# Moving one key-value block per pass next to the P blocks, and the ends of phi's softmax into the left places

## The chip, the cores and the metric

The kernel runs on one core of a Trainium2 chip. The metric is the device time of one execution in microseconds. A core has TensorE (matrix products; PE in the profile, its weight loads PEld), DVE (VectorE, elementwise work and reductions), ACT (ScalarE, activation functions and copies), POOL (GpSimd, used here for a few transfers) and SP (SyncE, which issues most transfers). Matmuls write to PSUM, which has eight banks.

## The reference

Attention through 32 memory slots for each head, then a feed-forward network with Silu, all in float32:

```python
a   = softmax(phi, axis=memory)             # 8 batches, 8 heads, 576 positions, 32 slots
k_m = einsum('bhsm,bhsd->bhmd', a, k)       # keys and values gathered into the slots
v_m = einsum('bhsm,bhsd->bhmd', a, v)
attn = softmax(q @ k_m.T / sqrt(64))        # 576 x 32 for each head
x   = attn @ v_m                            # then (4608, 512)
h   = x @ w_in                              # (4608, 2048)
out = (h * sigmoid(h)) @ w_out              # (4608, 512)
```

## The kernel before

Each of the eight batches is one pass over its 576 rows. For a batch the kernel multiplies the values with the input weights first (P = v_m times w_in, tile pm, four blocks of 512 columns), so that the first layer of the network is attention (tile aparts) times P. Every operand of a large product is split into a high and a low float32r part, and three of the four products of parts are added up.

A pass has 16 places, numbered 0 to 15. In passes 2 to 7 a place is one *step*: `ffn1s` makes h, the Silu input, for two chunks of 128 columns and half of the rows (12 matmuls at L846); `forms` evaluates Silu on ACT (L858, L860) and makes the operands of the second layer on ACT and DVE (L869 to L881); the place's other work (`run`) is issued; then `finish` issues the second layer of the step before (`st_step`, 21 matmuls at L894). That layer uses Strassen's seven products instead of eight; the combined weights it needs, `kept`, are made once from the sum of the weight parts (`w_sums` fetches that sum by transfers on POOL's queue, `w_forms` combines and splits it on DVE and ACT) in the course of passes 1 and 2. Pass 0 and the first ten places of pass 1 use plain products.

512 of the 576 rows of each batch go through these steps. The other 64 rows of two successive batches are kept in gleft and worked through together at the end of passes 1, 3, 5 and 7, in four *left places* with the numbers 16 to 19: `left_split` copies and splits a quarter of gleft (L978 on ACT, L979 on DVE), `run` issues the place's other work, and `finish` issues the matmuls of the *preceding* left part (`left_st`, L996). The fourth left part's matmuls come in the first step of the next pass.

Beside this, pass b prepares batch n = b + 1. Its pieces are put into the places by `ev(pass, place, function, ...)`, for passes 2 to 6 in `steady`:

- phi's softmax: `phi_max` and the three steps of `phi_fold` find a maximum on DVE, `phi_sub` subtracts it (DVE, L312 and L315), `phi_exp` takes the exponential (ACT, L319). Exponential and Silu are in different tables of ACT, so each exponential has a table load ahead of it and another one behind.
- `e_mm`, the key-value block: 80 small matmuls on 32-column tiles of TensorE (L335, L345), then rs and kvn on DVE and ACT (L353 to L361). It writes to the tile bg (`banks`) or to unused columns beside h (`beside_h`).
- `e_tr` and `s_all`: transposes and the scores (L382), which DVE turns into sc (L389, L391); then the softmax `s_max` ... `s_norm`; then `s_back` turns sc back (L464, DVE), `s_high` copies the high part into aparts (L472, ACT) and `s_low` the low part (L479, DVE).
- `p_mm`, a P block: 16 matmuls on 32-column tiles (L648) to bg or to two tiles pacc, then a copy on ACT (L676) and a subtraction on DVE (L678).

For n that is even (passes 1, 3, 5), `s_back`, `s_high` and `s_low` of the first half stand in the fourth left place (19) of passes 3 and 5; in pass 1 they stand in places 16 to 18. The third left place (18) has two P blocks. The two other P blocks come in the next pass: both in place 0 if that pass is even, in places 0 and 4 if it is odd.

The order on the engines: TensorE and, from pass 1 on, ACT are held to the order in which the program text issues their instructions (`in_order`). DVE and SP are ordered by the planner of the framework, with single order edges from `behind(i, other)`: in `run`, a DVE instruction of most functions comes behind the last split of the step (`last_split`) and behind the P subtractions issued in that place (`last_p`). `run` sorts the functions of a place: P blocks first, `w_forms` last.

Of the kernel before, what the change touches and what calls it, by code (L numbers as in the profile page):

```python
# [19 lines left out]
P = 128  # L20
# [28 lines left out]
def attn_ffn_kernel(  # L49
# [69 lines left out]

    raws, cvas, last_silu, last_split, last_kvn, last_turn = {}, {}, [], [], [], []  # L120
    raw_at = iter(range(1 << 30))
# [98 lines left out]
    def load_phi(b):  # L220
        t = sb.tile([P, PHW], F32, tag="y" if b == 2 else "x", name=f"phi{b}", bufs=1)
        at[b]["e"] = t[:, : FULLC * HM].rearrange("p (g c f) -> p g c f", g=2, c=FULLC)
        at[b]["er"] = t[:, FULLC * HM :]
        at[b]["et"] = t
        w = FULLC * P
        for f in ((0, w), (2 * w, PHW), (w, 2 * w)) if b == 0 else ((0, PHW),):
            load(t[:, f[0] : f[1]], phi[b, :, f[0] : f[1]], queue=nc.scalar if f[0] == w else None)
# [97 lines left out]
    def e_mm(b, cs=range(FULLC)):  # L325
        e, er, kvt, kr = (at[b][k] for k in ("e", "er", "kv", "kr"))
        if cs[0] == 0:
            at[b]["pt"] = beside_h(KVW) if b > 2 and b % 2 == 0 else banks(b)
        pt = at[b]["pt"]
# [42 lines left out]
    def s_all(b):  # L372

        sc = at[b]["sc"] = sb.tile([P, 2, S], F32, tag="x" if b == 2 else "y", name=f"sc{b}", bufs=1)
        bg, left = bgtile(), beside_h(S - 512)
        kvT = at[b]["kvT"]
        w = 512 - HALF
        for hf, f, n in ((0, 0, HALF), (1, 0, w), (1, w, HALF - w)):
            for r in range(NR):
                for p in range(2):  # L380
                    to = left[p] if f else bg[:, p, hf * HALF : hf * HALF + n]
                    nc.tensor.matmul(  # L382
                        to[M * r : M * (r + 1)],
                        kvT[D * p : D * (p + 1), 0, r],
                        at[b]["q", hf][D * p : D * (p + 1), r, f : f + n],
                        start=True, stop=True, skip_group_check=True,
                    )
        for p in range(2):
            ends = nc.vector.transpose(sc[:, p, 512:], left[p])  # L389
        for p in range(2):  # L390
            behind(nc.vector.transpose(sc[:, p, :512], bg[:, p]).ins, ends)  # L391

# [57 lines left out]
    def s_back(b, u, v=None):  # L450
# [3 lines left out]
        if u not in at[b]["aT"]:  # L454
            w = u[1] - u[0]
            tag = "cva" if b > 2 else ("x", "y")[b - 1]
            if b > 2 and b % 2 == 0 and u == FIRST:
                aT = gbuf[:, : 2 * w].rearrange("p (g s) -> p g s", g=2)
            else:
                aT = sb.tile([P, 2, w], F32, tag=tag, name=f"aT{b}", bufs=1)  # L460
            at[b]["aT"][u] = aT
# [273 lines left out]

    acc = {}

# [11 lines left out]
    def store(key, r):  # L749
        if key[0] == 0:  # L750
            o = raw_tile([P, DMODEL], F32, "o")
        else:
            o = shared[0][:, 1, key[1]]
        nc.scalar.activation(o, acc.pop(key), AF.Copy)
# [18 lines left out]
    kept, kept_at = [], []  # L773
    homes_left = [("w0", 4), ("w1", 4), ("w2", 4), ("w3", 4), ("r2", 4), ("kv2", 2), ("kv3", 2)]
    sum_homes = ("cva", 0, 1, "cva", 0, "y", "kv3", "cva")
    shared = []
# [31 lines left out]
    def w_forms(j, step):  # L808
        f = whole_sums[j]
        if step == 0:  # L810
            b11, b12, b21, b22 = (f[:, k, q * Q : (q + 1) * Q] for k in range(2) for q in range(2))
            for to, x, y, op in (
                (b11, b12, b11, ALU.subtract), (b12, b22, b12, ALU.add),
                (b22, b22, b11, ALU.add), (b21, b21, b22, ALU.subtract),
            ):
                behind(nc.vector.tensor_tensor(to, x, y, op=op).ins, last_split[-1])
            return
# [35 lines left out]
    def exp_slots(b):  # L853
        return () if b == B - 1 else (3, 10) if b == 1 else (4, 11) if b == 2 else (2, 11)

# [181 lines left out]
    def ev(b, slot, fn, *a):  # L1037
        events.setdefault((b, slot), []).append((fn, a))

    def steady(b, n):  # L1040


        early = b > 2
        if not early:
            ev(b, 1, phi_max, n)
            for i in range(3):
                ev(b, 2, phi_fold, n, i)
            ev(b, 3, phi_sub, n)
# [11 lines left out]
        ev(b, 12 if early else 11, s_sum, n, ALL)  # L1060
        ev(b, 13, s_norm, n, FIRST)
        turn = NFC + 3 if b % 2 else 14
# [5 lines left out]
        if b % 2:  # L1068
            ev(b, NFC, win_load, n, 3)
        for k in range(2):  # L1070
            ev(b, NFC + 2 if b % 2 else (13 if early else 12 + k) + k, p_mm, n, k * JW, JW, True, b % 2 and k)
        m = n + 1
        if m < B:
            ev(b, ex + 3, load_kv, m, range(2))
            ev(b, ex + 3, load_phi, m)
            ev(b, ex + 6, load_kv, m, range(2, FULLC))
            ev(b, 7 if early else 12, phi_max, m)
            for i in range(3):
                ev(*divmod(NFC * b + (11 + i if early else (13, 14, 16)[i]), NFC), phi_fold, m, i, load)
            ev(b + 1, 1, phi_sub, m)  # L1080

    SUMS = (
        (15, 35, 36), (33, 36, 37), (34, 38, 39), (36.5, 39, 40), (37.5, 40.5, 41.5), (39, 42, 44),
        (41, 50, 66), (65, 69, 71),
    )

    for b in range(B):
# [44 lines left out]
        ev(b, em, e_mm, n)  # L1132
        ev(b, 14 if b == 0 else em + 1, load_kv, n + 1, range(FULLC if b == 0 else 2))
        ev(b, tr, e_tr, n)
# [18 lines left out]
        ev(b, sk if n == 1 else NFC + 2, s_low, n, ALL)  # L1153
        ev(b, sk, load_phi, n + 1)
        if b == 0:
            ev(b, 14, p_mm, n, 0, JW)
# [142 lines left out]
    def run(b, slot):  # L1299
        todo = events.pop((b, slot), [])  # L1300
        turned = [e for e in todo if e[0] is p_mm] and [e for e in todo if e[0] is s_back]
        todo.sort(key=lambda e: 0 if e in turned else 1 if e[0] is p_mm else 3 if e[0] is w_forms else 2)
        last_p.clear()
        for fn, a in todo:
            n = len(nc.cur_bb.bb.instructions)
            fn(*a)
            for i in list(nc.cur_bb.bb.instructions)[n:]:
                if i.engine == DVE and fn is p_mm and turned:
                    behind(i, last_turn[0])
                elif i.engine == DVE and fn not in (p_mm, s_all):  # L1310
                    for other in [last_split[-1]] + last_p:
                        behind(i, other)

    for b in range(B):
# [11 lines left out]
        for s in range(NFC if b == 1 else 0):  # L1326
# [10 lines left out]
            for part in range(2):  # L1337
                for fn, a in events.pop((b, s + part / 2), []):
                    n = len(nc.cur_bb.bb.instructions)
                    fn(*a)  # L1340
                    for i in list(nc.cur_bb.bb.instructions)[n:]:
                        if i.engine == DVE and fn in (s_max, s_sub, s_sum, s_norm, s_back, s_low):
                            behind(i, last_split[-1])
                        elif i.engine == DVE and fn in (phi_max, phi_fold):
                            behind(i, last_p[-1])
            finish(range(NI))
# [87 lines left out]
```

## Time and profile before

| | |
|---|---|
| median of 3 runs | 675.34 us (675.12 to 675.85) |
| the profiled execution, time | 674.95 us |
| its span, first to last instruction | 673.1 us |
| PE busy | 664.0 us (99%) |
| DVE, ACT busy | 514.3 us (76%), 381.3 us (57%) |
| transfers | 98.11 MB, mean 146 GB/s |

In a timeline each row has the start (us from the span's start), the duration, engine, line, operation, out<-in, the shape and the count of merged instructions; brackets hold the engine's idle time before it and what ended it. A window row has the window, its length, then for PE, PEld, DVE, ACT and POOL the busy time and number of instructions, the granted TensorE clock (1.00 is full), the share of the transfer engines and GB/s. Matmuls overlap, so their durations are longer than their spacing.

### The profile page before, as it was taken

How to read it: one execution, taken by the hardware profiler on the slowest of the kernel's cores; microseconds unless marked ns; L12 is line 12 of the kernel's file. 1: busy time of each engine (PE TensorE's matmuls, PEld its weight loads, DVE VectorE, ACT ScalarE, POOL GpSimd, SP SyncE). 2: the span in 40 equal slices, each digit the busy share in tenths (PEclk: the TensorE clock that was granted, in tenths of full speed). 3: DMA queues.
4: the chain of work that ended last, by engine and by line, in shares of the span. 5: the costliest groups of instructions: out<-in, count | busy, mean ns of one | idle time of the engine just before them, and what ended most of it. 6: DMA issues, size and time to landing. Idle time of an engine off the chain costs nothing.

```text
span 673.1 us, 14669 instructions
## 1 busy us (share of the span) xinstructions
PE 664.0 (99%) x5846; PEld 590.7 (88%) x5846; DVE 514.3 (76%) x1101; ACT 381.3 (57%) x710; POOL 12.3 (2%) x22
## 2 busy tenths in 40 slices
PE   8999999999999999999999999999999999999997
PEld 3578777889979999999988999899997999889996
DVE  4997896758889799778877688877886667867654
ACT  3878685646546555644645546664654646554441
POOL 0000001120000000000000000000000000000000
PEclk9999999999999999999999999999999999999999
DMA  9998985497313551254420544225430204300001
GB/s 344 372 343 277 319 334 162 103 285 255 127 66 79 190 216 65 79 200 140 146 94 17 185 136 149 78 72 195 157 135 24 88 1 157 115 28 18 33 1 47
DMA packets 37043, 98.11 MB, mean 146 GB/s; under 512 B 4592, under 2 KB 19824, under 8 KB 33392
## 3 DMA queue, kind: packets, MB, share of 16 engines
q1 hardware_dynamic: 33648, 86.02, 36.5%
q0 software_dynamic: 2304, 8.39, 4.9%
q10 hardware_dynamic: 1024, 2.77, 1.1%
q8 instruction: 46, 0.75, 0.4%
q14 instruction: 21, 0.17, 0.1%
HBM read 75.12 MB, written 13.63 MB: 132 GB/s over the span
## 4 chain that ended last, share of the span: by engine, by line
PE 85%; DMA 2%; DVE 2%; ACT 2%; issue 1%; DVEq 0%
PE sum L894 41%; PE h L846 25%; PE lsum L996 6%; PE bg L648 3%; PE acc L745 3%; PE h L700 2%; DMA wfs<-wo_hi 1%; PE pacc L648 1%; DMA wfs<-wo_lo 1%; PE bg L335 1%; PE bg L382 1%; PE h L335 1%; ACT gbuf L858 0%; DVE kept L831 0%; PE lsum L1018 0%
## 5 line engine op out<-in xcount | busy, mean ns | idle before, releaser
L846 PE MATMUL h<-aparts,pm 128*128 128x288 f32 x1344 | 196.6, 295 | 0.2 <-DVE sc L389 0.2
L846 PEld LDWEIGHTS h<-aparts,pm 128*128 128x128 f32 x1344 | 184.4, 188 | 2.1 <-PE sum L894 0.6
L858 ACT ACTIVATE gbuf<-h 128x512 f32<-128x512 f32 x112 | 66.9, 597 | 137.1 <-PE h L846 135.0
L894 PE MATMUL sum<-wo_hi,aparts 128*128 128x256 f32 (+1 forms) x416 | 110.8, 290 | 0.0
L894 PE MATMUL sum<-wo_lo,aparts 128*128 128x256 f32 (+1 forms) x412 | 107.2, 283 | 0.0
L894 PE MATMUL sum<-kept,aparts 128*128 128x256 f32 x612 | 106.4, 282 | 0.0
L894 PE MATMUL sum<-wo_hi,gparts 128*128 128x256 f32 (+1 forms) x480 | 98.1, 299 | 0.0
L879 ACT ACTIVATE aparts<-gbuf 128x512 fp32r<-128x512 f32 x91 | 57.6, 632 | 68.4 <-DVE gbuf L874 68.4
L870 DVE TENSOR_TENSOR gbuf<-gbuf 128x256 f32<-128x256 f32 x102 | 43.1, 423 | 64.8 <-ACT gbuf L858 64.3
L894 PEld LDWEIGHTS sum<-kept,aparts 128*128 128x128 f32 x612 | 87.6, 191 | 0.2 <-DVE oo L953 0.2
L894 PEld LDWEIGHTS sum<-wo_hi,aparts 128*128 128x128 f32 x416 | 78.6, 189 | 10.1 <-ACT gleft L860 7.5
L894 PEld LDWEIGHTS sum<-wo_hi,gparts 128*128 128x128 f32 x480 | 76.3, 190 | 3.3 <-ACT gparts L715 0.8
L881 DVE TENSOR_TENSOR gparts<-gbuf,aparts 128x512 fp32r<-128x512 f32 x91 | 63.0, 692 | 20.6 <-ACT aparts L879 20.5
L894 PEld LDWEIGHTS sum<-wo_lo,aparts 128*128 128x128 f32 x412 | 78.4, 190 | 0.2
L894 PE MATMUL sum<-kept,gparts 128*128 128x256 f32 x306 | 69.8, 282 | 0.0
L869 ACT ACTIVATE aparts<-gbuf 128x384 fp32r<-128x384 f32 x102 | 53.6, 525 | 0.0
L894 PEld LDWEIGHTS sum<-kept,gparts 128*128 128x128 f32 x306 | 51.0, 191 | 0.0
L880 DVE TENSOR_TENSOR gparts<-gbuf,aparts 128x384 fp32r<-128x384 f32 x91 | 50.1, 550 | 0.0
L678 DVE TENSOR_TENSOR pm<-bg,pm 128x1024 fp32r<-128x1024 f32 (+1 forms) x29 | 31.0, 1070 | 9.8 <-ACT pm L676 9.8
L745 PE MATMUL acc<-wo_hi,gparts 128*128 128x512 f32 x128 | 36.9, 396 | 0.0
L873 DVE TENSOR_TENSOR gbuf<-gbuf 128x128 f32<-128x128 f32 x102 | 29.7, 291 | 3.0
L874 DVE TENSOR_TENSOR gbuf<-gbuf 128x128 f32<-128x128 f32 x102 | 29.5, 289 | 3.3
(223 smaller groups left out, 917.4 us busy)
## 6 DMA issues: line engine op xcount, KB each, us to landing
win<-win_saved SPq DMA_DIRECT2D x24, 1024.0 KB, 4.8
kv<-in_kv SPq DMA_DIRECT2D x28, 516.0 KB, 7.1
q<-in_q SPq DMA_DIRECT2D x16, 576.0 KB, 6.4
raw<-in_w_in SPq DMA_DIRECT2D x14, 512.0 KB, 7.6
raw<-in_w_out SPq DMA_DIRECT2D x6, 1024.0 KB, 7.1
win_saved<-win SPq DMA_DIRECT2D x4, 1024.0 KB, 8.5
phi<-in_phi SPq DMA_DIRECT2D x7, 576.0 KB, 8.7
out<-oo SPq DMA_DIRECT2D x26, 128.0 KB, 1.7
```

What stands on the lines that cost most here:

```text
L678: i = nc.vector.tensor_tensor(lo[:, g, c], bg[:, :, :w], hi[:, g, c], op=ALU.subtract)
L745: nc.tensor.matmul(acc[key], gt[:, cs], wt[:, fc], start=fc == 0 and n == 0, stop=fc == NFC - 1 and n == 2)
L846: nc.tensor.matmul(h[:, i, :HALF], wt[:, p, f : f + P], a[:, p], start=n[i] == 0, stop=n[i] == 5, skip_group_check=low_last,)
L858: nc.scalar.activation(to.rearrange("p (i f) -> p i f", i=2), h[:, :, :w], AF.Silu)
L869: nc.scalar.activation(hi[:, :3], g[:, 1:4], AF.Copy)
L870: nc.vector.tensor_tensor(g[:, 4:6], g[:, :1].broadcast_to([P, 2, P]), g[:, 1:3], op=ALU.subtract)
L873: nc.vector.tensor_tensor(g[:, 6], g[:, 1], g[:, 5], op=ALU.subtract)
L879: nc.scalar.activation(hi[:, 3:], g[:, 4:], AF.Copy)
L880: behind(nc.vector.tensor_tensor(lo[:, :3], g[:, 1:4], hi[:, :3], op=ALU.subtract).ins, s4)
L881: last_split.append(nc.vector.tensor_tensor(lo[:, 3:], g[:, 4:], hi[:, 3:], op=ALU.subtract))
L894: nc.tensor.matmul(sums[bank][:, cols], gt, wt, start=bank not in begun, stop=True, skip_group_check=True,)
L996: nc.tensor.matmul(sums[1 if b == 1 and fc > 11 else k], part[gt][:, 2 * i + k], wt[:, fc], start=n == 0 and i == 0 and m == 0, stop=True, ...
```

## The change

- `e_mm` of batches 3, 5 and 7 moves to place 0 of passes 2, 4 and 6 (from place 5 in pass 2 and 3 in passes 4 and 6), where two P blocks are, and writes beside h and no longer to bg. DVE's part of it no longer has to follow the P subtractions of that place; the subtractions of the block in pacc follow kvn.
- `phi_sub` and `phi_exp` of these batches move to the second and third left place (17, 18) of passes 1, 3 and 5, from places 3 and 4 of pass 2 and 1 and 2 of passes 4 and 6. A one-column Silu on the tile tiny follows the exponential. Batch 3's phi load, maximum and fold move into pass 1.
- In the even passes `e_tr` and `s_all` move to places 4 and 6. The exponential's place 2 (4 in pass 2) no longer counts as an exponential place of these passes, so `forms` there uses ACT again for one copy.
- Pass 2 follows the same places as passes 4 and 6 in all of `steady` (maximum in 7, folds in 11 to 13, P blocks in 13 and 14).
- `w_sums` and `w_forms` get new places (`SUMS`); sums 5 and 7 and the tiles `aT2` and `phi3` get other homes, the output of two stores another tile. The first half of `w_forms` for sum 4 is put behind the turn of the scores (`last_sc`).

```diff
-        t = sb.tile([P, PHW], F32, tag="y" if b == 2 else "x", name=f"phi{b}", bufs=1)
+        t = sb.tile([P, PHW], F32, tag="y" if b in (2, 3) else "x", name=f"phi{b}", bufs=1)
...
-            at[b]["pt"] = beside_h(KVW) if b > 2 and b % 2 == 0 else banks(b)
+            at[b]["pt"] = beside_h(KVW) if b > 2 else banks(b)
...
         for p in range(2):
-            behind(nc.vector.transpose(sc[:, p, :512], bg[:, p]).ins, ends)
+            last_sc[:] = [nc.vector.transpose(sc[:, p, :512], bg[:, p])]
+            behind(last_sc[0].ins, ends)
...
-            tag = "cva" if b > 2 else ("x", "y")[b - 1]
+            tag = "cva" if b > 2 else ("x", "r2")[b - 1]
...
-            o = shared[0][:, 1, key[1]]
+            if not key[1]:
+                staged.append(sb.tile([P, 2, DMODEL], F32, tag="kv2", name="o", bufs=1))
+            o = staged[0][:, key[1]]
...
-    homes_left = [("w0", 4), ("w1", 4), ("w2", 4), ("w3", 4), ("r2", 4), ("kv2", 2), ("kv3", 2)]
-    sum_homes = ("cva", 0, 1, "cva", 0, "y", "kv3", "cva")
+    homes_left = [("w0", 4), ("w1", 4), ("w2", 4), ("w3", 4), ("kv2", 2), ("r2", 4), ("kv3", 2)]
+    sum_homes = ("cva", 0, 1, "cva", 0, 1, "kv3", "x")
...
-                behind(nc.vector.tensor_tensor(to, x, y, op=op).ins, last_split[-1])
+                i = nc.vector.tensor_tensor(to, x, y, op=op).ins
+                behind(i, last_split[-1])
+                if j == 4:
+                    behind(i, last_sc[0])
...
-        return () if b == B - 1 else (3, 10) if b == 1 else (4, 11) if b == 2 else (2, 11)
+        return () if b == B - 1 else (3, 10) if b == 1 else (2, 11) if b % 2 else (11,)
...
+    def warm_silu():
+        nc.scalar.activation(tiny[:, :1], ident[:, :1], AF.Silu)
+
+    def phi_end(b, m):
+
+        ev(b, NFC + 1, phi_sub, m)
+        ev(b, NFC + 2, phi_exp, m)
+        ev(b, NFC + 2, warm_silu)
+
     def steady(b, n):
-        early = b > 2
-        if not early:
-            ev(b, 1, phi_max, n)
-            for i in range(3):
-                ev(b, 2, phi_fold, n, i)
-            ev(b, 3, phi_sub, n)
-        ex = exp_slots(b)[0]
-        em = ex + 1 + b % 2
-        ev(b, ex, phi_exp, n)
+        odd = b % 2
+        if odd:
+            ev(b, 2, phi_exp, n)
+        em, tr, sa = (4, 6, 7) if odd else (0, 4, 6)
         ev(b, em, e_mm, n)
...
-        ev(b, ex + 4 - (not early), e_tr, n)
-        ev(b, ex + 5 - (not early), s_all, n)
+        ev(b, tr, e_tr, n)
+        ev(b, sa, s_all, n)
...
-            ev(b + 1, 1, phi_sub, m)
+            if odd:
+                phi_end(b, m)
+            else:
+                ev(b + 1, 1, phi_sub, m)
 
     SUMS = (
-        (15, 35, 36), (33, 36, 37), (34, 38, 39), (36.5, 39, 40), (37.5, 40.5, 41.5), (39, 42, 44),
-        (41, 50, 66), (65, 69, 71),
+        (15, 35, 35.5), (33, 36, 36.5), (34, 37, 37.5), (36, 39, 40), (37, 40.5, 41.5), (38, 42, 43),
+        (41, 65, 66), (49, 67, 68),
     )
...
+            ev(b, 9, load_phi, n + 1)
+            ev(b, 12, phi_max, n + 1)
+            for i in range(3):
+                ev(b, 13 + i, phi_fold, n + 1, i, load)
+            phi_end(b, n + 1)
...
+                elif i.engine == DVE and fn is p_mm and a[4:] == (True,):
+                    beside.append(i)
                 elif i.engine == DVE and fn not in (p_mm, s_all):
-                    for other in [last_split[-1]] + last_p:
+                    for other in last_split[-1:] if fn is e_mm and slot == 0 else [last_split[-1]] + last_p:
                         behind(i, other)
+            if fn is e_mm and slot == 0:
+                for i in beside:
+                    behind(i, last_kvn[0])
```

More of the change, by code (lines that the diff above doesn't have):

```diff
@@ L116, in bgtile @@
         return ps.tile([P, 2, 512], F32, tag="bg", name="bg", bufs=1)
-    raws, cvas, last_silu, last_split, last_kvn, last_turn = {}, {}, [], [], [], []
+    raws, cvas, last_silu, last_split, last_kvn, last_turn, last_sc = {}, {}, [], [], [], [], []
     raw_at = iter(range(1 << 30))
@@ L734, in silu @@
         return g32
-    acc = {}
+    acc, staged = {}, []
     def ffn2(gs, cs, fc, key, terms=(0, 1, 2)):
@@ L1059, in steady @@
         ev(b, 11, s_exp, n, ALL)
-        ev(b, 12 if early else 11, s_sum, n, ALL)
+        ev(b, 12, s_sum, n, ALL)
         ev(b, 13, s_norm, n, FIRST)
-        turn = NFC + 3 if b % 2 else 14
+        turn = NFC + 3 if odd else 14
         ev(b, turn, s_back, n, FIRST)
@@ L1067, in steady @@
             ev(b, 10 + 2 * k, win_load, n, k)
-        if b % 2:
+        if odd:
             ev(b, NFC, win_load, n, 3)
         for k in range(2):
-            ev(b, NFC + 2 if b % 2 else (13 if early else 12 + k) + k, p_mm, n, k * JW, JW, True, b % 2 and k)
+            ev(b, NFC + 2 if odd else 13 + k, p_mm, n, k * JW, JW, True, odd and k)
         m = n + 1
         if m < B:
[L1074 to L1077, printed above, removed]
+            ev(b, 5, load_kv, m, range(2))
+            ev(b, 5, load_phi, m)
+            ev(b, 8, load_kv, m, range(2, FULLC))
+            ev(b, 7, phi_max, m)
             for i in range(3):
-                ev(*divmod(NFC * b + (11 + i if early else (13, 14, 16)[i]), NFC), phi_fold, m, i, load)
-            ev(b + 1, 1, phi_sub, m)
+                ev(b, 11 + i, phi_fold, m, i, load)
+            if odd:
+                phi_end(b, m)
+            else:
+                ev(b + 1, 1, phi_sub, m)
     SUMS = (
-        (15, 35, 36), (33, 36, 37), (34, 38, 39), (36.5, 39, 40), (37.5, 40.5, 41.5), (39, 42, 44),
-        (41, 50, 66), (65, 69, 71),
+        (15, 35, 35.5), (33, 36, 36.5), (34, 37, 37.5), (36, 39, 40), (37, 40.5, 41.5), (38, 42, 43),
+        (41, 65, 66), (49, 67, 68),
     )
@@ L1132, in attn_ffn_kernel @@
         ev(b, em, e_mm, n)
-        ev(b, 14 if b == 0 else em + 1, load_kv, n + 1, range(FULLC if b == 0 else 2))
+        ev(b, 14 if b == 0 else 8, load_kv, n + 1, range(FULLC if b == 0 else 2))
         ev(b, tr, e_tr, n)
@@ L1153, in attn_ffn_kernel @@
         ev(b, sk if n == 1 else NFC + 2, s_low, n, ALL)
-        ev(b, sk, load_phi, n + 1)
         if b == 0:
+            ev(b, sk, load_phi, n + 1)
             ev(b, 14, p_mm, n, 0, JW)
@@ L1303, in run @@
         last_p.clear()
+        beside = []
         for fn, a in todo:
@@ L1341, in attn_ffn_kernel @@
                     for i in list(nc.cur_bb.bb.instructions)[n:]:
-                        if i.engine == DVE and fn in (s_max, s_sub, s_sum, s_norm, s_back, s_low):
+                        if i.engine == DVE and s < NP and fn in (phi_max, phi_fold):
+                            behind(i, last_p[-1])
+                        elif i.engine == DVE and fn in (s_max, s_sub, s_sum, s_norm, phi_max, phi_fold, phi_sub):
                             behind(i, last_split[-1])
-                        elif i.engine == DVE and fn in (phi_max, phi_fold):
-                            behind(i, last_p[-1])
             finish(range(NI))
```

## The prediction, made before the result was known

> **What bounds the kernel now.** I read the page first, then the timelines of TensorE, ACT and DVE around each stretch that the diff edits.
>
> ```profile
> span 673.1 us, 14669 instructions
> PE 664.0 (99%) x5846; PEld 590.7 (88%) x5846; DVE 514.3 (76%) x1101; ACT 381.3 (57%) x710; POOL 12.3 (2%) x22
> ```
>
> TensorE is busy for 664.0 of 673.1 us, and the change neither adds nor removes a matmul. So the time can move in three ways: a cheaper order of the same matmuls, a stall that goes, a stall that comes. A stall of TensorE, once taken, is not earned back, because no slack follows it. Whole steps show the first two. In the next view each window runs from the first h matmul of one step to that of the next; the length is the first number, TensorE's busy time the second (the counts take in one or two matmuls of the neighbours).
>
> ```profile
> 364.48:368.59 4.11, 4.11 (x35) 4.11 (x34) 3.77 (x9) 2.37 (x5) 0.00 (x0) 1.00 0.16 38
> 368.59:375.17 6.58, 6.58 (x115) 6.02 (x114) 4.15 (x11) 4.38 (x7) 0.00 (x0) 1.00 0.47 162
> 419.01:424.31 5.30, 5.30 (x51) 4.29 (x50) 3.96 (x9) 1.98 (x5) 0.00 (x0) 1.00 0.14 49
> 446.03:453.63 7.60, 7.60 (x131) 6.20 (x130) 6.10 (x18) 3.70 (x7) 0.00 (x0) 1.00 0.39 116
> 274.15:278.62 4.47, 4.42 (x35) 4.19 (x34) 4.37 (x11) 2.35 (x6) 0.00 (x0) 1.00 0.21 72
> 231.92:237.70 5.78, 5.66 (x83) 4.79 (x82) 4.93 (x13) 3.72 (x10) 0.00 (x0) 1.00 0.39 127
> 387.69:393.16 5.47, 5.47 (x84) 4.77 (x82) 3.49 (x10) 2.05 (x5) 0.00 (x0) 1.00 0.38 111
> 121.59:125.92 4.33, 4.33 (x26) 3.85 (x25) 4.15 (x10) 2.51 (x4) 0.00 (x0) 1.00 0.87 164
> 146.00:152.04 6.04, 5.85 (x73) 4.40 (x72) 4.92 (x13) 3.06 (x7) 1.18 (x2) 1.00 1.05 183
> ```
>
> **Part 1: the key-value block joins P.** A bare step is 4.11 us. With the key-value block alone it is 6.58 (2.47 more), with one P block alone 5.30 (1.19), with both side by side 7.60 (3.49). Side by side saves 2.47 + 1.19 - 3.49 = 0.17 us: one passage from full tiles to 32-column tiles and back less. Batches 4 and 6 have that already; the change gives it to 3, 5 and 7: **-0.5 us**. The block now writes beside h, as it does at 446.03 without a stall. Behind it in the first step lie 12 matmuls of the last left part before h is wanted again, and its few DVE operations go ahead of the pacc splits by a new order edge, so I cost its evacuation at nothing. If that cover failed, the rest of a step like the 0.36 us below would be the price.
>
> **Part 2: three stalls that go.** At 274.15 a step without any block takes 4.47, 0.36 over the bare one: the sums of the batch before are read late, because the last phi fold stands on DVE in that step; the fold moves back to places 11 to 13, where passes 4 to 6 have it. -0.36. At 231.92 the score block of batch 3 costs 5.78 against 5.47 of the same step in pass 4; ACT copied the last key's forms just before. Those forms move to places 3 and 4, the scores to 6: -0.31. At 146.00 the score block costs 6.04 - 4.33 = 1.71 over its neighbour, against 5.47 - 4.11 = 1.36: 0.35 lost. There DVE turned the scores (L389) only after the forms:
>
> ```profile
> 150.31 0.42 DVE L816 TENSOR_TENSOR wfs<-wfs 128x256 f32<-128x256 f32 x1 [0.20 <-DMA wfs<-wo_lo]
> 150.66 0.95 DVE L831 TENSOR_TENSOR kept<-wf,kept 128x768 fp32r<-128x768 f32 x1
> 151.52 0.37 DVE L389 STREAM_TRANSPOSE sc<-h 128x64 f32<-128x64 f32 x2
> ```
>
> The new edge puts the forms of sum 4 behind the turn: -0.35. Together **-1.0 us**. The lower bound of this part is zero, if other work takes those places: passes 1 and 2 get phi's maximum and the last two sums' forms in full steps (DVE is busy 3.77 of 4.11 even in the quiet step above).
>
> **Part 3: phi's last parts in the left places.** phi_sub moves to the second left place, phi_exp to the third, with a tiny Silu behind it that reloads the table. ACT executes in written order; its row at 349.58 below shows it: the copy of the fourth left part reads gleft, long written, yet it ran after the P copies and not in the 2.46 us of idle time before them. The third place writes the P copies first, then phi_exp and the tiny Silu; only then come the fourth place's copy (L978) and s_high (L472). This is the end of pass 3, first ACT, then DVE, then TensorE.
>
> ```profile
> 347.71 1.02 ACT L676 ACTIVATE pm<-bg 128x1024 fp32r<-128x1024 f32 x1 [2.46 <-PE bg L648]
> 348.63 1.08 ACT L676 ACTIVATE pm<-pacc 128x512 fp32r<-128x512 f32 x2
> 349.58 0.65 ACT L978 ACTIVATE aparts<-gleft 128x512 fp32r<-128x512 f32 x1
> 352.56 0.69 ACT L472 ACTIVATE aparts<-gbuf 128x576 fp32r<-128x576 f32 x1 [2.33 <-DVE gbuf L464]
> 355.75 0.60 ACT L858 ACTIVATE gbuf<-h 128x512 f32<-128x512 f32 x1 [2.50 <-PE h L846]
> ```
>
> ```profile
> 349.90 1.28 DVE L678 TENSOR_TENSOR pm<-pacc,pm 128x512 fp32r<-128x512 f32 x2
> 351.10 0.68 DVE L979 TENSOR_TENSOR aparts<-gleft,aparts 128x512 fp32r<-128x512 f32 x1
> 351.70 0.83 DVE L464 STREAM_TRANSPOSE gbuf<-sc 128x288 f32<-128x288 f32 x2
> 353.28 0.76 DVE L479 TENSOR_TENSOR aparts<-gbuf,aparts 128x576 fp32r<-128x576 f32 x1 [0.75 <-ACT aparts L472]
> ```
>
> ```profile
> 353.97 1.74 PE L846 MATMUL h<-aparts,pm 128*128 128x288 f32 x12
> 355.64 1.09 PE L648 MATMUL bg<-win,kvT 64*32 64x512 f32 x16
> 356.52 1.06 PE L648 MATMUL pacc<-win,kvT 64*32 64x512 f32 x16
> ```
>
> The chain is: copy L978, its difference L979, the turn L464 (written behind L979), s_high L472, s_low L479, then h of the next pass, whose first two matmuls need s_high and whose third needs s_low. The third starts about 353.97 + 2 x 0.14 = 354.25; s_low ends at 354.04. That is 0.2 us of slack. L978 ended at 350.23 and L979 waited for the pacc splits until 351.10: another 0.85. So ACT may slip **about 1.05 us** here before TensorE feels it. What the exponential takes on ACT:
>
> ```profile
> 367.45 1.28 ACT L319 ACT_TABLE_LOAD   x1
> 368.74 1.17 ACT L319 ACTIVATE phi<-phi 128x1152 f32<-128x1152 f32 x1
> 369.94 1.28 ACT L858 ACT_TABLE_LOAD   x1
> 371.23 0.60 ACT L858 ACTIVATE gbuf<-h 128x512 f32<-128x512 f32 x1
> ```
> ```profile
> L1224 ACT ACTIVATE tiny<-ident x1: 202/202/202, 21.3 to 21.3; 128x1 f32<-128x1 f32 x1
> ```
>
> From load to the next activation 371.23 - 367.45 = 3.78 us, with the second load in it 1.28 + 0.01 + 1.17 + 0.03 + 1.28; I add the tiny Silu's 0.20 and 0.15 for overlap with the P copies that is lost: 4.1 us. L978 would end at 354.4 in place of 350.2, L464 run from 355.0, s_high to 356.6, s_low to 357.3: h comes 4.1 - 1.05, **about 3.1 us late**. Queued behind are only what follows in order; Silu of the next step waits for h anyway. It happens at the ends of passes 3 and 5; pass 5 ends in the same way, with the same gaps:
>
> ```profile
> 508.76 0.65 ACT L978 ACTIVATE aparts<-gleft 128x512 fp32r<-128x512 f32 x1
> 511.74 0.69 ACT L472 ACTIVATE aparts<-gbuf 128x576 fp32r<-128x576 f32 x1 [2.33 <-DVE gbuf L464]
> ```
>
> Together **+6.2 us**. The bounds of one such stall: 1.5, if DVE turned the scores before L979 after all (s_high is then held by ACT alone, to 354.95, and s_low ends 1.7 later than now); 5.1, if phi_sub's DVE operations came after the P splits and not in DVE's idle time before them, 2.0 more by
>
> ```profile
> L312 DVE TENSOR_TENSOR phi<-phi,am x12: 676/680/687, 122.8 to 525.2; 128x512 f32<-128x512 f32 x12
> L315 DVE TENSOR_TENSOR phi<-phi,am x12: 276/284/291, 123.4 to 525.9; 64x128 f32<-64x128 f32 x12
> ```
>
> two of each, 1.9 us. I take 3.1, since phi_sub is written before them and its operands are there. In pass 1 the same edit costs nothing: s_high stands a place earlier there, and ACT idles longer than 4.1 us before the next Silu:
>
> ```profile
> 195.97 0.60 ACT L858 ACTIVATE gbuf<-h 128x512 f32<-128x512 f32 x1 [5.58 <-PE h L846]
> ```
>
> The exponential that leaves the second place of passes 4 and 6 frees ACT where TensorE doesn't wait for it: nothing (the step at 364.48 and the one at 368.59, which holds it, have no idle time of TensorE). The moved loads (phi, key-value, the sums' transfers) are wanted several steps after their new places: nothing. In pass 1 the fold's seven small moves for batch 3 leave DVE and pass through SP's queue between the P window loads; if they waited there, the fourth window would be late for the first step of pass 2. Passes 2 to 5 send them in this way already, and no step there has idle time of TensorE for it: nothing.
>
> The Trainium skill, "ScalarE: Activation LUTs", section "What ACT_TABLE_LOAD costs", gives 2.66 us for a switch, 1.28 of load and 1.38 of drain. This trace has the 1.28 and no drain (0.01 to 0.03 us on either side); by the page's figure each stall would be 2.8 us longer and the time 685.5 us, which I leave out.
>
> **The sum.** -0.5 - 1.0 + 6.2 = +4.7 us. The profiled execution took 674.95 us (its span 673.1 and 1.85 around it), so 679.6; it is 0.39 below the median of 675.34, and on the median the sum is **680.0 us**.
>
> **Rivals.**
> (a) *The clock drops in the new gap.* After the last matmul, ended 669.27, the granted clock fell to a half at about 671.94, 2.7 us later:
>
> ```profile
> 668.00:669.30 1.30, 1.27 (x11) 1.06 (x9) 1.01 (x3) 0.26 (x1) 0.00 (x0) 1.00 0.00 0
> 669.30:671.50 2.20, 0.00 (x0) 0.00 (x0) 0.51 (x2) 0.00 (x0) 0.00 (x0) 1.00 0.44 102
> 671.50:672.00 0.50, 0.00 (x0) 0.00 (x0) 0.00 (x0) 0.00 (x0) 0.00 (x0) 0.94 0.37 76
> ```
>
> The new gaps (2.4 us, two matmuls, 0.6 us) are just shorter. If the clock stayed low for as long as such a gap, some 3 us, 1.5 us are lost each: 681.5 with one, 683.0 with both. Trainium skill, "TensorE: Matmul & The Clock Gate", "HAM oscillation": only idle gaps over about 3.4 us throttle; by that rule this rival is out, by the row it is not.
> (b) *DVE turns the scores ahead of L979*: the lower bound, 675.34 - 1.5 + 2 x 1.5 = 676.8. Against it: L464 followed L979 although DVE idled earlier with sc ready.
> (c) *Not slower: ACT takes phi's exponential after s_high.* This decides if the planner's order on ACT isn't the written one. s_high ends at 353.25; 4.1 us more reach 357.35, 1.6 past the Silu's 355.75; the P blocks of the first step, in whose shadow it may lie, end at 357.6, so its end at 358.1 delays the key-value block by 0.5: 675.34 - 1.5 + 1.0 = 674.8, or 673.8 if the exponential is fully hidden. It holds as long as the slip before L978 stays under the 1.05 us. The row at 349.58 speaks against it.
> (d) *New lateness on DVE in the filled steps of passes 1 and 2* beside the forecast: the -1.0 is lost and two stalls of the 0.36 kind come, 681.7.
>
> **How the numbers follow.** Forecast 0.60 (its own range 679.0 to 681.8: each stall 2.6 with all of part 2, or 3.5 with none), (a) 0.14, (b) 0.07, (c) 0.12, (d) 0.07. The range from (b) to just over (a) with both gaps, 676.8 to 683.5, leaves out (c) and the upper bound of phi_sub. A measurement of this kernel tells 0.2%, 1.35 us, from no change: (c) splits into 0.07 faster and 0.05 same; slower 0.88.
>
> **What would show it.** Right: at the ends of passes 3 and 5 a table load behind the P copies, L978 ending some 4 us later against them, and TensorE idle before h for s_high and s_low, 3 us in all; none at the end of pass 1. Steps with P and the key-value block adding 2.3 and not 2.5 us; no 4.47 step. Wrong: h following the third left part at once, an exponential that stands elsewhere on ACT, or a granted clock under 1.00 in the middle of the span.

## The result and the profile after

| | before | after |
|---|---|---|
| median of 6 runs each | 675.12 us (674.75 to 675.85) | 685.24 us (683.30 to 686.54) |
| ratio, 95% interval | | 1.0146 (1.0129 to 1.0163) |
| the profiled execution | 674.95 us | 683.30 us |

The change makes the kernel 1.5% slower, 10.1 us on the medians. The forecast was 680.0 us with a range of 676.8 to 683.5: the direction is right, the size isn't, and the time lies outside the range. The profiled execution is the fastest of the six; what sets it apart turns out to be the clock.

First the head of the page of after: span, busy times, the row of the granted clock in 40 slices, and the group of the h matmuls with TensorE's idle time before it and what ended most of it.

```profile
span 681.5 us, 14667 instructions
...
PE 666.0 (98%) x5846; PEld 591.9 (87%) x5846; DVE 512.4 (75%) x1093; ACT 383.8 (56%) x715; POOL 12.2 (2%) x22
...
PEclk9999999999999999999999999999998999999999
...
L852 PE MATMUL h<-aparts,pm 128*128 128x288 f32 x1344 | 198.8, 297 | 6.2 <-ACT aparts L473 4.7
```

There are as many matmuls as before. 6.2 us of idle time now stand before the h matmuls, 4.7 of them ended by ACT's s_high (L473), and the slice that begins at 511 us has a clock below the others. Then the windows of after, from the first h matmul of one step to that of the next, with the same columns as in the prediction. The first four rows are the last left places of pass 3 with the first step of pass 4, then the same of pass 5 and 6; two rows from pass 2 and three from pass 1 follow.

```profile
338.12:357.52 19.40, 17.05 (x124) 13.57 (x122) 13.57 (x29) 11.76 (x19) 0.00 (x0) 1.00 0.23 82
357.52:366.89 9.37, 9.10 (x137) 6.38 (x137) 6.12 (x15) 4.42 (x9) 0.00 (x0) 1.00 0.35 118
500.23:519.62 19.39, 17.05 (x125) 13.57 (x123) 13.59 (x29) 11.76 (x19) 0.00 (x0) 1.00 0.23 82
519.62:530.46 10.84, 10.58 (x137) 7.43 (x138) 6.39 (x15) 4.42 (x9) 0.00 (x0) 0.84 0.23 76
...
225.53:230.96 5.43, 5.43 (x84) 4.79 (x83) 3.70 (x10) 2.27 (x5) 0.00 (x0) 1.00 0.61 199
275.54:279.66 4.12, 4.12 (x36) 4.12 (x34) 3.94 (x9) 2.39 (x6) 0.00 (x0) 1.00 0.20 66
...
126.18:130.77 4.59, 4.50 (x25) 3.65 (x23) 2.82 (x6) 3.86 (x7) 0.55 (x1) 1.00 0.01 2
146.64:152.33 5.69, 5.69 (x73) 4.55 (x72) 3.45 (x8) 2.90 (x6) 1.73 (x2) 1.00 1.05 233
161.03:166.17 5.14, 4.27 (x35) 4.07 (x33) 4.52 (x11) 3.15 (x5) 0.00 (x0) 1.00 0.78 288
```

The same steps of before are these: the left places of pass 3 and the first step of pass 4, then the steps of pass 1 that answer to 126.18 and 161.03.

```profile
337.07:353.97 16.90, 16.90 (x125) 13.74 (x123) 12.47 (x25) 7.83 (x15) 0.00 (x0) 1.00 0.27 94
353.97:360.39 6.42, 6.42 (x58) 4.36 (x56) 3.56 (x8) 3.95 (x8) 0.00 (x0) 1.00 0.00 0
125.92:130.26 4.34, 4.34 (x25) 3.84 (x24) 1.50 (x4) 3.16 (x6) 0.00 (x0) 1.00 0.00 0
160.79:164.91 4.12, 4.12 (x35) 4.11 (x34) 3.56 (x8) 3.54 (x5) 0.00 (x0) 1.00 0.36 88
```

Step by step the profiled execution accounts for itself as follows, against the profile of before. A first step with P and the key-value block and without a stall takes 8.73 us in the profiles of two of the experiments (turn_early and turn_late_phi3, below), 0.16 less than 6.42 + 2.47.

| where | difference |
|---|---|
| start and pass 0, up to 120 us (differs between executions by up to 1 us) | +0.3 |
| pass 1: +0.24 and +1.03 at the two steps of the rows above (from start to start, where the rows round), +0.12 in the step between (6.94 for 6.81), +0.56 in its last steps and left places; 6.04 to 5.69 | +1.9 - 0.35 |
| pass 2: 4.47 to 4.12, 5.78 to 5.43 | -0.7 |
| key-value block beside P: 0.07 in pass 2, 0.16 in passes 4 and 6; 0.06 at the scores of these two | -0.5 |
| end of pass 3: 19.40 for 16.90, 9.37 for 8.73 | +3.1 |
| end of pass 5: 19.39 for 16.90, 10.84 for 8.73 | +4.6 |

Together 8.35, which is the difference of the two profiled executions. The end of pass 3 after the change, ACT, DVE and TensorE in turn (timelines; start, duration, engine, line):

```profile
350.78 1.28 ACT L319 ACT_TABLE_LOAD   x1
352.07 1.17 ACT L319 ACTIVATE phi<-phi 128x1152 f32<-128x1152 f32 x1
353.26 1.28 ACT L1047 ACT_TABLE_LOAD   x1
354.56 0.20 ACT L1047 ACTIVATE tiny<-ident 128x1 f32<-128x1 f32 x1
354.67 0.61 ACT L984 ACTIVATE aparts<-gleft 128x512 fp32r<-128x512 f32 x1
356.79 0.68 ACT L473 ACTIVATE aparts<-gbuf 128x576 fp32r<-128x576 f32 x1 [1.51 <-DVE gbuf L465]
```
```profile
355.32 0.69 DVE L985 TENSOR_TENSOR aparts<-gleft,aparts 128x512 fp32r<-128x512 f32 x1 [2.72 <-ACT aparts L984]
355.93 0.83 DVE L465 STREAM_TRANSPOSE gbuf<-sc 128x288 f32<-128x288 f32 x2
357.50 0.76 DVE L480 TENSOR_TENSOR aparts<-gbuf,aparts 128x576 fp32r<-128x576 f32 x1 [0.75 <-ACT aparts L473]
```
```profile
357.52 0.53 PE L852 MATMUL h<-aparts,pm 128*128 128x288 f32 x2 [2.35 <-ACT aparts L473]
```

This is the chain that the prediction laid out. The table loads and the exponential stand between the P copies and the copy of the fourth left part; DVE idles 2.72 us for that copy, turns the scores behind it, and TensorE waits 2.35 us for s_high. Its third h matmul starts only at 358.32, after another 0.26 us for s_low.

At the end of pass 5 there is more. The next rows are windows cut where the granted clock changes (the last number but two is the clock).

```profile
353.21:356.63 3.42, 1.96 (x9) 1.31 (x7) 1.31 (x3) 2.04 (x4) 0.00 (x0) 1.00 0.00 0
...
517.05:520.47 3.42, 0.83 (x5) 0.36 (x3) 2.20 (x4) 1.01 (x2) 0.00 (x0) 1.00 0.00 0
520.47:523.88 3.41, 3.41 (x18) 2.56 (x26) 0.06 (x1) 0.69 (x3) 0.00 (x0) 0.50 0.02 5
```

From 520.47 to 523.88 TensorE runs at half its clock: 3.41 us in which it does the work of 1.7. The gap that went before is no longer than the one at the end of pass 3, after which the clock stays at 1.00. Single executions bear this out: the two fastest of after, 683.30 and 683.93 us, have a mean clock of 0.997, the four others, 685.14 to 686.54 us, of 0.994 or 0.995. One such drop takes half of 3.41 us, 0.25% of the span, off the mean clock; so I read one drop in the former and two in the latter. The drop behind the last matmul is in these means too, but takes little: at most 0.15% in the profiles (2.05 us in turn_early, below). This is a reading of means: the profile of after shows one drop directly, two stand in the profiles of two of the experiments, and one of 13 executions of before had 0.997 as well, at 675.96 us.

The lateness of pass 1 in the waits of after (what waits, what it waits for, us in total, times, the longest), and then in its timeline:

```profile
DVE wfs L819 <- DMA wfs<-wo_lo: 2.0, 1, 2.0
```
```profile
155.22 1.80 DVE L819 TENSOR_TENSOR wfs<-wfs 128x256 f32<-128x256 f32 x4 [2.02 <-DMA wfs<-wo_lo]
...
164.11 1.28 ACT L864 ACT_TABLE_LOAD   x1 [1.98 <-DVE gparts L883]
...
166.17 1.86 PE L852 MATMUL h<-aparts,pm 128*128 128x288 f32 x12 [0.87 <-ACT gleft L866]
```

DVE stands 2.02 us until the transfer of a weight sum (sum 4) has landed. Its operands for the second layer then come late, ACT waits 1.98 us for them at 164.11, its Silu runs late, and TensorE stands 0.87 us for a part of h that ACT still has to read out.

### The profile page after: what moved, and what is told of

Same layout as the page of the kernel before. It is cut to its first block, busy times and chain, and to the rows that moved or that the text cites. A ratio compares the mean times of both kernels' runs of the same rounds, so it can differ in the third digit from the quotient of the medians.

```text
span 681.5 us, 14667 instructions
## 1 busy us (share of the span) xinstructions
PE 666.0 (98%) x5846; PEld 591.9 (87%) x5846; DVE 512.4 (75%) x1093; ACT 383.8 (56%) x715; POOL 12.2 (2%) x22
## 4 chain that ended last, share of the span: by engine, by line
PE 78%; DVE 5%; ACT 4%; DMA 3%; issue 1%; DVEq 0%; ACTq 0%
PE sum L900 38%; PE h L852 24%; PE lsum L1002 5%; PE bg L649 3%; PE acc L746 3%; PE h L701 2%; DMA wfs<-wo_hi 2%; PE h L335 1%; DMA wfs<-wo_lo 1%; PE bg L382 1%; ACT pm L677 1%; ACT L319 1%; PE pacc L649 1%; DVE wfs L819 0%; ACT L1047 0%
## 5 line engine op out<-in xcount | busy, mean ns | idle before, releaser
L852 PE MATMUL h<-aparts,pm 128*128 128x288 f32 x1344 | 198.8, 297 | 6.2 <-ACT aparts L473 4.7
L885 ACT ACTIVATE aparts<-gbuf 128x512 fp32r<-128x512 f32 x94 | 59.4, 632 | 70.1 <-DVE gbuf L880 70.1
L887 DVE TENSOR_TENSOR gparts<-gbuf,aparts 128x512 fp32r<-128x512 f32 x94 | 65.1, 692 | 21.4 <-ACT aparts L885 21.4
L886 DVE TENSOR_TENSOR gparts<-gbuf,aparts 128x384 fp32r<-128x384 f32 x94 | 51.8, 551 | 0.0
L677 ACT ACTIVATE pm<-bg 128x1024 fp32r<-128x1024 f32 (+1 forms) x29 | 26.0, 896 | 10.5 <-PE bg L649 10.4
L880 DVE TENSOR_TENSOR gbuf<-gbuf 128x128 f32<-128x128 f32 x102 | 29.4, 289 | 3.3
```

Source lines behind the costliest of these rows:

```text
L677: nc.scalar.activation(hi[:, g, c], bg[:, :, :w], AF.Copy)
L852: nc.tensor.matmul(h[:, i, :HALF], wt[:, p, f : f + P], a[:, p], start=n[i] == 0, stop=n[i] == 5, skip_group_check=low_last,)
L885: nc.scalar.activation(hi[:, 3:], g[:, 4:], AF.Copy)
L886: behind(nc.vector.tensor_tensor(lo[:, :3], g[:, 1:4], hi[:, :3], op=ALU.subtract).ins, s4)
L887: last_split.append(nc.vector.tensor_tensor(lo[:, 3:], g[:, 4:], hi[:, 3:], op=ALU.subtract))
```

## The experiments

Each edit is against the kernel after; each time is compared with runs of the kernel before on the same chip. The ratio is to before, with its 95% interval.

**The gap filled (gap_filled).** Eleven matmuls of an unused product run on TensorE after the last left place of passes 3 and 5, so that it isn't idle while it waits; they write nothing that is read.

```diff
+            if 1 < b < B - 1:
+                keep_warm(bgtile()[:, 0], 11)
```

> The changed kernel with 11 dummy matmuls on TensorE at the end of passes 3 and 5, in the gap before h; nothing else differs, and the dummies' results are read by nobody. Theory A (two stalls of 3.2 us each, and on top of them the clock falls to a half for 3.4 us behind one or both gaps, 1.5 to 1.7 us each): the stall of h for s_high and s_low stays, the granted clock stays 1.00 until the last matmul, and all executions come out near 683.3 - 1.5 = 681.8 us with a spread under 1 us. Rival B (the spread of 683.3 to 686.5 us between executions has another cause than the gap): median near 685.2 us as before, same spread.

682.01 us (681.26 to 682.46), ratio 1.0096 (1.0081 to 1.0111). TensorE at the end of pass 3:

```profile
354.53 2.55 PE L80 MATMUL bg<-ident 128*128 128x512 bf16 x11
357.03 0.53 PE L852 MATMUL h<-aparts,pm 128*128 128x288 f32 x2
```

h waits as long as before. The first step of pass 6 now is

```profile
519.07:528.41 9.34, 9.08 (x138) 6.39 (x137) 6.08 (x15) 4.42 (x9) 0.00 (x0) 1.00 0.27 87
```

at full clock, 1.50 us shorter than the 10.84 of after, and the median falls by 3.2 us, about two such drops. The clock is a cost of its own, beside the stall that brings it on.

**No tiny Silu (no_warm).** The table goes back to Silu's only with the next Silu; the copies in between don't need it.

```diff
-        ev(b, NFC + 2, warm_silu)
```

> The changed kernel without the tiny Silu behind phi's exponential, so that the Silu table is loaded only ahead of the next pass's first Silu. Theory A (h waits for ACT's written order, with a slip of 4.1 us of which 1.05 are free): the copy of the fourth left part starts 1.28 + 0.20 = 1.5 us earlier, each stall shrinks from 3.2 to 1.7 us, the gap gets too short for the clock: 683.3 - 1.5 - 3.0 = 678.8 us, no clock under 1.00. Rival B (the stall is due to DVE, phi_sub ahead of the P splits): the stalls stay at 3.2 us and the time within 1 us of 685.2.

679.75 us (679.07 to 679.99), ratio 1.0062 (1.0047 to 1.0077). ACT, then TensorE:

```profile
353.39 1.17 ACT L319 ACTIVATE phi<-phi 128x1152 f32<-128x1152 f32 x1
354.47 0.61 ACT L984 ACTIVATE aparts<-gleft 128x512 fp32r<-128x512 f32 x1
```
```profile
357.32 0.53 PE L852 MATMUL h<-aparts,pm 128*128 128x288 f32 x2 [0.83 <-ACT aparts L473]
```

The copy follows the exponential at once, and the gap shrinks from 2.35 to 0.83 us: 1.52 less, for a table load of 1.28 and an activation of 0.20. After so short a gap the clock didn't drop. Of the 5.5 us of the median, 3.0 are the two stalls; the other 2.5 go with the drops. The second table load now starts at 358.13 us and costs nothing, since ACT waits for h there. The result is 1 us above the expectation; half of that stands in the step of pass 1 that takes 5.14 us after the change and took 5.67 here, which differs between executions (see late_phi3).

**The scores turned before the exponential (turn_early).** `s_back`, `s_high` and `s_low` move from place 19 to place 17.

```diff
-        turn = NFC + 3 if odd else 14
+        turn = NFC + 1 if odd else 14
```

> The changed kernel with s_back, s_high and s_low of the first half in the second left place of passes 3 and 5 and no longer in the fourth, so that they stand ahead of phi's exponential on ACT. Theory A: no stall of h at the ends of passes 3 and 5 and no drop of the clock, 683.3 - 1.5 - 6.3 = 675.5 us; what is left of the difference to before (gains 0.5 + 0.7 + 0.3 us against some 1.8 us lost in pass 1) is about nothing. Rival B (the exponential in the left places costs by itself, by DVE's and ACT's load there): a new stall takes the old one's place and the time stays above 678 us.

676.10 us (675.45 to 677.05), ratio 1.0012 (1.0002 to 1.0022). ACT, then TensorE:

```profile
349.09 0.68 ACT L473 ACTIVATE aparts<-gbuf 128x576 fp32r<-128x576 f32 x1 [1.84 <-DVE gbuf L465]
```
```profile
356.49 1.74 PE L852 MATMUL h<-aparts,pm 128*128 128x288 f32 x12
```

s_high is done 6.7 us before h wants it. The left places take 16.90 us and the first step 8.73, and the clock stays at 1.00 until after the last matmul. This one edit takes away 9 of the 10 us. The exponential itself takes as long as before; only what stood behind it has moved.

**Batch 3's phi loaded late (late_phi3).** The load of pass 1 waits for the turn of the scores; Sync issues it at 153.01 us and no longer at 135.41 (before the change it was at 184.11).

```diff
+            if b == 3:
+                tc.add_manual_dep(loads[-1].ins, last_sc[0].ins.name, ...)
```

> The changed kernel with the load of batch 3's phi held back until the scores of batch 2 are turned (about 153 us), where it was issued at 135.4 us. For the 1.7 us that pass 1 loses. Theory C (that load crowds the weight sums' transfers, sum 4 comes 2.5 us late and with it DVE's s_max, s_sub and the forms of place 10): the 5.14 us step at 161 us falls to 4.1 to 4.3 and the time by 1.0 to 1.5 us, to about 684.0 us. Rival D (the sums' new places and their order in POOL's queue do it): the step stays at about 5.1 us and the time at 685.2.

684.09 us (683.42 to 684.81), ratio 1.0128 (1.0113 to 1.0143). The step of pass 1, then DVE's wait:

```profile
160.77:165.00 4.23, 4.23 (x34) 4.06 (x33) 3.63 (x9) 3.15 (x5) 0.00 (x0) 1.00 1.03 420
```
```profile
DVE wfs L826 <- DMA wfs<-wo_lo: 1.1, 1, 1.1
```

5.14 becomes 4.23, and DVE's wait for the weight sum 2.0 becomes 1.1: the 0.9 us. The profiles of four other experiments, whose programs don't differ from after up to this step, show how the step follows that wait: 4.73 us with a wait of 1.60 (gap_filled), 5.67 with 2.51 (no_warm), 5.73 with 2.58 (turn_early) and 5.82 with 2.65 (exp_behind_high). In each, and with the load late too, the step is 3.1 to 3.2 us longer than the wait. So the size of this cost changes from execution to execution, 0.6 to 1.7 us over the bare 4.11, and 0.9 is one sample of what the late load saves; the medians give 1.15. The phi load (128x1152 float32) at 135 us, which the prediction costed at nothing, thus costs about 1 us at 161 by making a weight sum late, though not by itself: old_sums, below, brings the step down with the load left at 135. How it does so isn't fully shown: POOL's longest wait, 8.1 us for the high half of a sum, is the same in both. In this profile both gaps are followed by a drop of the clock.

```profile
353.34:356.75 3.41, 1.06 (x5) 0.46 (x3) 1.93 (x4) 1.38 (x3) 0.00 (x0) 1.00 0.00 0
356.75:360.17 3.42, 3.16 (x19) 2.65 (x26) 0.26 (x1) 0.30 (x1) 0.00 (x0) 0.50 0.00 0
```

**Both (turn_late_phi3).**

> Both edits that helped alone: s_back, s_high and s_low of passes 3 and 5 in the second left place, and batch 3's phi load held back behind the turn of batch 2's scores. If the two costs are independent, 676.1 - 1.2 = 674.9 us, a hair faster than before (675.0), and no step of pass 1 at 161 us over 4.3. If the load only hides another cause in pass 1, 676 us.

675.18 us (674.29 to 675.89), ratio to before 0.9997 (0.9988 to 1.0006), before at 675.30: no difference.

```profile
338.12:355.01 16.89, 16.89 (x124) 13.74 (x123) 13.58 (x28) 11.43 (x19) 0.00 (x0) 1.00 0.27 95
355.01:363.74 8.73, 8.73 (x137) 6.24 (x136) 6.00 (x15) 4.68 (x10) 0.00 (x0) 1.00 0.40 129
```

With the two causes gone, the ends of passes 3 and 5 cost nothing. The gains of parts 1 and 2, 1.5 us, are there, and pass 1 gives back 1.1 of them in small pieces: 0.24 and 0.12 at the steps of 126 and 131 us, 0.18, 0.10, 0.25 and 0.20 later.

**The old places of the first sums (turn_both, old_sums, combined).** The 0.36 us at 126 and 131 looked like the forms of the first three sums, which the change puts half a place or more earlier. ACT after the change, then ACT before it:

```profile
127.85 0.85 ACT L836 ACTIVATE kept<-wf 128x768 fp32r<-128x768 f32 x1 [0.70 <-DVE wf L819]
128.71 1.28 ACT L864 ACT_TABLE_LOAD   x1
```
```profile
127.74 1.28 ACT L858 ACT_TABLE_LOAD   x1 [1.17 <-PE h L846]
```

Before the change the table load for Silu waited for h alone; now it stands behind a copy of the sum's form, which DVE had made late. `turn_both` is turn_late_phi3 with the old places of the first six sums; `old_sums` is the kernel after with those alone; `combined` is turn_both with the last of them a place earlier.

```diff
-        (15, 35, 35.5), (33, 36, 36.5), (34, 37, 37.5), (36, 39, 40), (37, 40.5, 41.5), (38, 42, 43),
+        (15, 35, 36), (33, 36, 37), (34, 38, 39), (36.5, 39, 40), (37.5, 40.5, 41.5), (39, 42, 44),
```

> The same with the first six sums back at their old places (the last two, for pass 2, stay at the new ones). Theory E (the new, earlier place 3.5 of the first forms puts ACT copies ahead of the Silu table's load in the exponential's place 3, and two steps there lose 0.24 + 0.12 us): these steps return to 4.35 and 6.81 us, 674.9 - 0.4 = 674.5 us. Rival F (in their old places the forms of sum 5 meet phi's maximum, now in place 12 of pass 1, and DVE is late there): a step at places 12 to 14 loses as much or more, 674.9 us or above.

> The changed kernel with the first six sums back at their old places alone. Theory E: the steps at 126 and 131 us return to 4.35 and 6.81 us. For the 1 us at 161: theory C (the phi load crowds the transfers) leaves it at 4.5 to 5.7 us, theory D (the sums' order in POOL's queue) takes it to 4.1.

> The changed kernel with s_back, s_high, s_low of passes 3 and 5 in the second left place, batch 3's phi load held back, the first five sums at their old places, sum 5 asked for at its old place and its second forms at the new one (place 11 of pass 1). Theory E with DVE free enough: the two steps at 126 and 131 us stay at 4.35 and 6.81 us, no step of places 10 to 13 is over 4.4 us, 675.2 - 0.5 = 674.7 us, 0.1% faster than before. Rival F (DVE is full in places 10 to 13 of pass 1 once phi's maximum and folds of batch 3 are there, wherever the sums' forms go): 0.3 to 0.8 us come back there, 675.2 us or above.

| | time | ratio |
|---|---|---|
| turn_both | 675.94 us (675.46 to 677.27) | 1.0015 (1.0006 to 1.0023) |
| old_sums, one run | 684.85 us | |
| combined | 676.06 us (675.27 to 677.53) | 1.0014 (1.0005 to 1.0023) |

In old_sums the steps at 126 and 131 are back at the times of before, 4.35 and 6.81, and the step at 161 is too (window):

```profile
161.24:165.35 4.11, 4.11 (x35) 4.11 (x33) 2.15 (x4) 3.53 (x5) 0.00 (x0) 1.00 0.67 146
```

What is gained there comes back later. In old_sums the step at 165.35 takes 4.62 us for 4.11; in turn_both the step at 173.85 takes 4.59 us for 4.11 and the left places 17.63 for 16.90; in combined the steps at 165.08 and 170.17 take 5.09 and 5.00. There sum 5 is the late one, DVE waits 2.3 us for its transfer. Both turn_both and combined so come out on the side of their rival F, and the gain that was expected of them is missing.

The forms of six sums, phi's maximum and its fold have to go through DVE in some ten steps. Each order tried makes another of them late; that DVE has too little room there is my reading of this and not shown by itself. Which part of the step at 161 belongs to the phi load and which to the new order of the sums isn't settled either: undoing one of the two is enough to bring it down, so it takes both together.

**Phi's maximum later as well (combined_later).** In combined, the maximum of batch 3 goes to place 14 of pass 1, the fold to 14, 15 and 16.

```diff
-            ev(b, 12, phi_max, n + 1)
-            for i in range(3):
-                ev(b, 13 + i, phi_fold, n + 1, i, load)
+            ev(b, 14, phi_max, n + 1)
+            for i in range(3):
+                ev(b, (14, 15, 16)[i], phi_fold, n + 1, i, load)
```

> As the kernel just described, with batch 3's maximum two places later (14 for 12) and its folds one place later each (14, 15, 16). Rival F: DVE has room in places 11 to 13, their steps are 4.11 to 4.2 us, and 0.3 us are saved against it, 674.4 to 674.9 us. If the room is missing in the left places too (DVE has phi_sub, s_low and the sums' evacuation there), the lateness moves there and the time is 675.2 us or above.

680.56 us (677.80 to 682.95), ratio 1.0084 (1.0063 to 1.0105), a miss. The waits say why:

```profile
PE h L859 <- DVE aparts L487: 1.9, 1, 1.9
DVE wide L310 <- DMA fm<-fm: 1.9, 1, 1.9
```

DVE waits 1.9 us for the small moves of the fold, s_low of batch 2 stands behind that, and h of the first step of pass 2 waits the same 1.9 us. With a stall of TensorE of that length the times spread over 5 us, and the mean clock is 0.999 in the two fastest executions and 0.992 to 0.997 in the others.

**The exponential behind s_high (exp_behind_high).** This is the order of rival (c): in passes 3 and 5 `phi_exp` and the tiny Silu move to place 19, behind `s_high`.

```diff
-        ev(b, NFC + 2, phi_exp, m)
-        ev(b, NFC + 2, warm_silu)
+        ev(b, NFC + (2 if b == 1 else 3), phi_exp, m)
+        ev(b, NFC + (2 if b == 1 else 3), warm_silu)
```

> The changed kernel with phi's exponential and the tiny Silu of passes 3 and 5 in the fourth left place behind s_high, in place of the third (the order that the prediction's rival (c) was about); pass 1 as changed. Theory A: h is no longer late at the ends of passes 3 and 5, the next Silu starts 1.6 us late, the key-value block behind it 0.5 us: 676.1 + 1.0 = 677.1 us. Rival G (the late Silu delays more, because P's copies on ACT and the release of their tiles follow it): a stall of over 1 us in the first two steps of passes 4 and 6, above 678 us.

677.98 us (677.24 to 678.49), ratio 1.0039 (1.0026 to 1.0053). ACT, then TensorE in the first step of pass 4:

```profile
359.69 0.58 ACT L864 ACTIVATE gbuf<-h 128x512 f32<-128x512 f32 x1
```
```profile
360.43 1.97 PE L335 MATMUL h<-kv,phi 128*32 128x129 f32 x64 [0.33 <-ACT gleft L866]
```

The exponential follows s_high, which had waited 2.70 us for the turn anyway; the Silu starts at 359.69, straight behind it. The key-value block, which writes beside h, waits for ACT to have read h out. The first step takes 9.43 us for 8.73: 0.70 us a pass, where the prediction had 0.5 for this place.

## Why the prediction was wrong

**The direction and the main term were right.** Part 3, the stalls of h at the ends of passes 3 and 5, was 3.1 us each and measured 3.1: 2.50 more in the left places and 0.64 in the first step (9.37 against 8.73). ACT's order, the table loads on both sides, the copy that waits and the turn behind it came as written; the copy ends at 354.67 + 0.61 = 355.28, 5.05 us later than in the old trace, of which 1.05 are the later start of the stretch: ACT slips 4.0 us where the working had 4.1. turn_early removes the stalls and no_warm shortens each by the load and the tiny activation alone. Rival (b), DVE turning ahead of L985, didn't happen (355.93 after 355.32), nor rival (c), which as a kernel of its own costs 0.70 a pass.

**Part 1 was nearly right**: 0.16 us in passes 4 and 6 for the 0.17 of the prediction (8.73 against 6.42 + 2.47), but 0.07 in pass 2; 0.4 in all for 0.5. **Part 2 was right**: 4.12 for 4.47, 5.43 for 5.78 and 5.69 for 6.04, three times 0.35.

**The first step that failed is the weight of rival (a).** The prediction saw that the new gaps are close to the one after which the clock fell at the end of the span, called them "just shorter" and gave the drop 0.14. What stood there was a delay of 2.7 us from the last matmul to the drop, read from one place and taken for a threshold. The runs show that the delay isn't a threshold. The clock drops at the ends of windows of 3.41 us that run on by themselves, and in these traces it follows how much of such a window TensorE was idle. In late_phi3 the drops begin at 356.75 and 520.59, in old_sums at 358.09 and 521.93: in both 163.84 us apart, 48.0 windows of 3.413, although the gaps are 163.26 us apart in the latter (the h matmuls start at 357.85 and 521.11). In after, 48 windows before 520.47 is 356.63, in the midst of the first gap: it was cut in two, TensorE was busy for 1.96 of the 3.42 us, and the clock stayed. Windows with 0.83 and 1.06 us busy were followed by a drop. The fall behind the last matmul obeys the same grid: in all twelve profiles each fall of the clock on record lies a whole number of windows behind the first record of the clock (in after that stands at 5.05 us, 515.42 us or 151.0 windows before the fall at 520.47). These last windows also narrow the share (first turn_early, then turn_both):

```profile
669.81:673.23 3.42, 1.51 (x13) 1.31 (x11) 1.51 (x4) 0.38 (x1) 0.00 (x0) 1.00 0.19 43
```
```profile
668.32:671.73 3.41, 1.84 (x14) 1.57 (x12) 1.51 (x4) 0.38 (x1) 0.00 (x0) 1.00 0.17 38
```

Behind the first the clock is 0.50, behind the second still 1.00. A gap of 2.6 us (2.35 and 0.26) can throttle or not by where the window falls; by its mean clock no execution of after was without a drop. By the price that the prediction gave, 1.5 us for one and 3.0 for both, this is the larger part of the miss.

The Trainium skill has the rule that the prediction set against this row: "TensorE: Matmul & The Clock Gate", section "HAM oscillation", by which only idle gaps over about 3.4 us throttle. As a rule for gaps this case doesn't bear it out: gaps of 2.6 us throttled, and filling them won 3.2 us. What agrees is the length: 3.41 us is that of the window here.

**The second is "the moved loads: nothing" and, for pass 1, the seven moves and full steps at nothing.** Pass 1 lost 1.9 us beside the 0.35 that it won as forecast. 1.03 of it stand in the step at 161: the late sum 4, which comes of the phi load moved to 135 us together with the sums' new order, since late_phi3 takes away 0.9 of it and old_sums all; 0.36 are the sums' forms in front of Silu, as old_sums shows; 0.6 are spread over its last steps and are only argued to be DVE's and ACT's backlog. Rival (d) had the mechanism, lateness in the filled steps of pass 1, but it came beside the gains of part 2 and not in their place. The prediction named the queue of the P windows and looked whether these would be late; the transfers of the weight sums, under way at the same time as the moved load and with the transfer engines fully busy (a share of 0.97 to 1.04 from 135.4 to 144 us), it left out.

**The range** took one rival at a time: the forecast with both drops, 683.0 us, was its upper end. The two failed steps add up: 680.0 + 1.9 + 1.5 or 3.0 gives 683.4 or 684.9 us, against means of 683.6 and 685.7 for the two groups of executions; 0.8 us of the latter is left without a cause. The 685.5 us that the prediction set aside, with a drain behind each table load, is near the median by luck: the trace has no such drain.

**What is open**: where between 44% (1.51 of 3.42 us) and 54% (1.84 of 3.41) of busy time in a window the clock decides, whether it goes by the busy time or by the longest idle piece in the window, which these runs don't tell apart, and how phi's load and the order of the sums together make sum 4 late.

## What to carry to other kernels

An engine that runs in written order makes everything behind a moved piece late by that piece: look at what stands behind the new place on the same engine, and move the urgent copy ahead of it (here one number, and 9 us). A stall of TensorE of some 2.5 us should be priced with the drop of the clock that may follow, 1.5 us more each, and two risks that can come at once belong into one range, added. A load moved earlier isn't free because its data is wanted late: see which transfers with a reader close by are under way at its new place.

## What the runs showed of the hardware

- The clock drop lasts one window of 3.413 us at 0.50 and ends by itself; windows start at a spacing of 3.413 us that doesn't follow the work (48.0 of them between two drops, twice). So a gap of 2.6 us costs a drop in one execution and not in another of the same kernel; by their mean clocks, the executions of after fall into two groups (683.6 and 685.7 us as the means).
- Windows at full clock in which TensorE was busy for 1.51 of 3.42 us or less were followed by a half clock, windows with 1.84 of 3.41 or more weren't.
- A gap of 0.83 us and the 0.26 after it never did this in the four executions of no_warm (mean clock 0.999 to 1.000).
- A table load on ACT runs without a drain in the kernel after as well: 350.78 + 1.28 is 352.06, and the exponential starts at 352.07.
